# A new issue order for sketched attention with a gated MLP: S2 on the sync queue, copies of S behind the second turn of keys

## The chip, the cores and the metric

The kernel runs on one core of a Trainium2 chip. The metric is the time of one execution on the device in microseconds; lower is better. The engines are named as in the profile: PE is TensorE (matmuls), PEld its weight loads, DVE is VectorE, ACT is ScalarE, POOL is GpSimd, and SP is SyncE, which issues nearly all DMAs. A "q" behind a name is the engine's sequencer.

## The reference

Sixteen pairs of batch and head (4 by 4), 1088 positions, head size 32, all float32. Each row of q and k is sketched by two 8x32 matrices, and the attention is linear in the 64 products:

```python
a = einsum('rd,bhsd->bhsr', S1, x)
b = einsum('rd,bhsd->bhsr', S2, x)
phi(x) = einsum('bhsi,bhsj->bhsij', a, b).reshape(..., 64)
kv  = einsum('bhsf,bhsd->bhfd', phi(k), v)
z   = sum(phi(k), axis=2)
out = einsum('bhsf,bhfd->bhsd', phi(q), kv) / (einsum('bhsf,bhf->bhs', phi(q), z)[..., None] + 1e-06)
```

The result, reordered to 4352 tokens of 128 features, goes through a gated MLP with 2048 hidden units:

```python
h = x @ w_in
g = h * (1.0 / (1.0 + exp(-beta * h)))
result = g @ w_out
```

## The kernel before

Every step of the work is a small function under a short name, put into a table by a decorator: `@op("l2")` or an entry `DO["tk1"]`. A string, SEQ, lists all names in the order in which the instructions are issued, and the last two lines run through it: `for s_ in SEQ.split(): DO[s_]()`. There is no scheduler behind it. Each engine executes its own instructions in just this order and waits at each for its operands and for the buffer that it writes; engines run ahead of one another as far as that allows. So SEQ sets both the queue of each engine and, by the case of a letter, often the engine itself: the same step exists in a form for VectorE (capital) and one for GpSimd or ScalarE (small letter).

The names, with their lines in the profile (a digit 0 to 3 behind a name is the batch b; a second digit a part of it):

- Loads, on SP unless said otherwise: l1 and l2 (S1 and S2, lines 216 and 220, on ACT's queue), lka and lkb (the two halves of the keys of b=0) and lk1 to lk3 (line 148), lq0 to lq3 (queries, 148), lv0 to lv3 (values, 163), lb0 and lb1 (beta, spread over the partitions, 184), li0 and li1 (w_in, 178), lo0 and lo1 (w_out, 192), lp (beta, one column per hidden unit, 224), vz (a memset of a value tile on GpSimd, 175).
- Start: ci and c0 (constants), c1 (head sums of the identity, DVE, 259), h0 and h (one filler matmul on constant data, 128x384, line 267, whose result nobody reads), sm (spread_s: S1 and S2 over the partitions by matmuls, 287 and 294, into one PSUM tile `sps`), sk (masked copies of it, ACT, 305), SW0/SW1 or sw0/sw1 (plain copies of it, DVE or ACT, 317), BS or bs (blocks of S2, DVE or ACT; bs is line 328).
- Keys and queries per batch: tka, tkb, tk1.. and tq0.. (32x32 turns on DVE, 494), kpa, kpb, kp1.. (the projections of the keys, 513), ka (turn of them into `kab`, DVE, 571), o/O (outer products of the keys, `kp`, in five parts, GpSimd or DVE, 536), gr (gram, 586), gc/GC (its copy, ACT or DVE, 597), wp (wprime, 606), wm0, wc/WC (copies of it, 618 and 694), qp and qc0 (projections of the queries, 513, 630 and 703), qa and qd0 (turns into `qab` and `qcc`, DVE, 641, 717 and 648).
- Denominator: DM/dm (product, DVE or GpSimd, 656 and 723), DR (sum, 670 and 732), DI (reciprocal, 674 and 737), DS/ds (scaling of `qab`, 678 and 741). For b=0 a and b are the first two and the other seven of nine groups of columns.
- p/P (outer products of the queries, `qo`, GpSimd or DVE, 536), in parts like o/O. For b=0 they are turned on PE (f0 to f4, line 864) and copied (m/M, ACT or DVE, 878); for the others they are turned on DVE (t, four parts per batch, 757).
- v (sums over the keys, PE, 838 for b=0 and 809), kc and kt (copy or turn of the result, 850 and 821), nd (six small DMAs that deal it out, SP, 507), n0x and n1 to n3 (the numerators, PE, 892 and 772), x/X (their copies to the tokens `xT`, ACT or DVE, 904, 783 and 790).
- MLP weights: u/U (w_in times beta, GpSimd or DVE, 339, four blocks of 512 columns, `winp`), rb (1/beta, DVE, 362), a/g/e (w_out times 1/beta, sixteen blocks, ACT, GpSimd or DVE, 345 and 353, `woutp`).
- MLP: W (1024 columns of h for a chunk of tokens, two or four matmuls, line 400, into one of two PSUM buffers `wave`), S (silu of one W on ACT, 417, into one of 24 tiles g), V (the second product for one W, 447; 435 for the last chunk), y (result out of PSUM, DVE, 470 and 467), z (stores, SP, 376 and 481). There are 68 each of W, S and V; W, S and V take the chunks in order (256, 512, 256, six of 512, 256 tokens), so that the first sixteen W need tokens of b=0 alone.

PSUM is cut into named buffers: two `wave` (two banks each), one `two` (two banks), one `one`, and one accumulator. sps, gram, wprime, kvs and n02 share `one`; kps, the first tile of qps, f1 to f4 and the first tile of n1 to n3 share `two`; the second tiles of qps and n1 to n3, and f0 with n00, take a `wave`. GpSimd can't reach PSUM here: all its steps are products of two SBUF tiles.

Of the kernel before, what the change touches and what calls it, by code (L numbers as in the profile page):

```python
# [19 lines left out]
def kernel(  # L20
# [14 lines left out]
    B, H, S, D = q.shape  # L35
# [50 lines left out]
    def sb(shape, dtype, name):  # L86
        return const.tile(shape, dtype, tag=name, name=name)
# [16 lines left out]
    PE, DVE, ACT, POOL, SP = nc.tensor, nc.vector, nc.scalar, nc.gpsimd, nc.sync  # L104
    DO = {}

    def op(name):
        def put(fn):
            assert name not in DO, name
            DO[name] = fn  # L110
            return fn

        return put
# [11 lines left out]
    sr = sb([R, 2, D], F32, "sr")  # L125
# [12 lines left out]
    sk = sb([P, 2, 2, R], F32, "sk")  # L138
# [78 lines left out]

    @op("l2")
    def load_s2():
        ACT.dma_start(out=sr[:, 1], in_=S2)  # L220

    @op("lp")
    def load_beta_pu():
# [659 lines left out]
    for n, (j0, j1) in enumerate(JRP):  # L883
# [20 lines left out]
                eng(out=xT[:, P * j0 : P * j0 + w], in_=b0["n", n][:, :w])  # L904

    SEQ = """
        ci l2 l1 h0 h h lka c0 tka h lkb h h h h sm h sk h SW0 tkb h kpa c1 h lq0 kpb lk1 lv0 lq1 bs ka0
        SW1 o00 tq0 h h h h gr0 h gc0 h wp0 wm0 o04 qp0 o01 lb0 o03 li0 qc0 tk1 qa0 qd0 DMa h DRa DMb
        o02 DIa DRb kp1 h v00 ka1 dsa v01 p00 h li1 DIb tq1 DSb gr1 gc1 v02 h lb1 h h wp1 f0 P04 P03 wc1
        qp1 P01 M0 v03 qa10 lv1 U0 v04 kc qa11 O10 p02 h u1 lp U3 h n00 f1 x00 f2 W h DM1 W lk2 h m1 m2  # L910
        lo0 n01 U2 S O11 S O14 f3 lo1 W O13 x01 DR1 DI1 rb W o12 v10 S f4 M3 S W v11 tk2 S v12 lk3 v13
        vz m4 v14 lq2 e7 h g0 DS1 W kt1 a1 nd1 g3 W kp2 S n02 g5 e13 g11 W e9 g4 g8 e2 a10 S ka2 V g14
        P10 W x02 e15 gr2 t10 S W S g6 V gc2 W S wp2 V e12 p11 tq2 WC2 t11 S V W qp2 y V qa20 lq3 lv2
        qa21 S p13 o20 W p12 V dm2 t13 V S t12 W W tk3 V V o21 S o22 n1 O24 V S W DR2 X10 o23 v20 v21
        v22 v23 DI2 x11 v24 ds2 S W V S W P20 lv3 kp3 S kt2 nd2 t20 W S V P22 ka3 W gr3 W S y S t22 P21
        V p23 GC3 z W t23 S z V W V t21 V S o30 W O33 S tq3 wp3 y WC3 n2 W S X20 o32 X21 v30 V V W S qp3
        qa30 V qa31 o31 W V V z S W S W S V V DM3 W DR3 V W v31 S v32 W y O34 DI3 S DS3 V W V S S W z
        p30 V W S V S W V W S p32 V W S V W p33 V S t30 y W v33 v34 S W S V W V S p31 S W V t32 t31 W S
        V S W V S kt3 W V W S V t33 V S nd3 y W n3 V X30 S V z V W V V S X31 W W V S V W V z S y W S S V
        W V S W V S W V W V V S W S W V V S S W S V W V S W S V W V W S V S W V y W S V S W S V W V S V  # L920
        V z y V z y z z
    """
    for s_ in SEQ.split():
        DO[s_]()
# [29 lines left out]
```

## Time and profile before

| | us |
|---|---|
| median of 3 runs | 110.5 (110.27 to 114.07) |
| the profiled execution | 110.41 |
| its span, first to last instruction | 108.6 |
| PE busy, share of the span | 97.3 (90%) |
| DVE busy | 64.0 (59%) |
| ACT busy | 71.7 (66%) |
| POOL busy | 35.4 (33%) |

All times in the rows are microseconds from the start of the span. A row of a timeline gives start, length, engine, line, operation, output and inputs, shapes and a count; where several like instructions follow one another they are one row, and its length runs from the first start to the last end. In brackets stands the idle time of the engine before it and what ended it. A row of the chain that ended last gives start, length and what the end of the program hung on at that time. A row of the table by windows gives the window, its length, then the busy time and the number of instructions of PE, PEld, DVE, ACT and POOL, then the granted TensorE clock, the share of the DMA engines and GB/s.

### The profile page before, as it was taken

What the parts mean: (1) busy time and instruction counts of PE and PEld (TensorE: products, weight loads), DVE (VectorE), ACT (ScalarE), POOL (GpSimd) and SP (SyncE); (2) the same over time, 40 slices, a digit from 0 to 9 for tenths busy, and PEclk for the clock granted to TensorE, in tenths of its full rate; (3) what the DMA queues carried; (4) which work ended last, traced back from release to release, by engine and by line L of the source; (5) the groups of instructions that cost most, each with busy time, mean ns of one, the idle gap of its engine ahead of it and who ended that gap; (6) DMA issues with size and microseconds to landing.
All of it is one profiled execution on the core that took longest, in us unless ns stands there. A gap on an engine that the chain in (4) does not pass through costs nothing.

```text
span 108.6 us, 2920 instructions
## 1 busy us (share of the span) xinstructions
PE 97.3 (90%) x1193; PEld 54.8 (50%) x1193; DVE 64.0 (59%) x120; ACT 71.7 (66%) x90; POOL 35.4 (33%) x50
## 2 busy tenths in 40 slices
PE   6798769599996989999999999999999999999930
PEld 3323446185743645655744555555554554556820
DVE  3269999999599999979984844037026220100210
ACT  3230001149897938389946699999991899999900
POOL 5009758800866707794900007900000000000000
PEclk9999999958999999999999999999999999999996
DMA  3999999999201698001354001400025405023061
GB/s 74 351 247 230 368 410 259 240 388 398 88 0 27 187 273 179 4 6 26 61 82 73 0 3 30 66 0 15 15 48 83 79 13 89 0 34 63 0 97 48
DMA packets 23660, 12.64 MB, mean 116 GB/s; under 512 B 19424, under 2 KB 21728, under 8 KB 23648
## 3 DMA queue, kind: packets, MB, share of 16 engines
q1 hardware_dynamic: 23616, 12.47, 44.4%
q8 instruction: 9, 0.15, 0.6%
q14 instruction: 3, 0.02, 0.1%
q10 hardware_dynamic: 32, 0.00, 0.0%
HBM read 9.94 MB, written 2.23 MB: 112 GB/s over the span
## 4 chain that ended last, share of the span: by engine, by line
PE 68%; DVE 21%; issue 3%; DMA 3%; ACTq 1%; DVEq 0%
PE wave L400 27%; PE moeout L447 24%; PE nps L772 4%; DVE woutp L353 4%; DVE qT L494 3%; PE kvs L809 3%; DMA sr<-in_S_dram 3%; PE qfps L864 3%; DVE qo L536 3%; DVE kT L494 2%; DVE kab L571 2%; PE kps L513 2%; PE moeout L435 2%; DVE qm L656 1%; PE kvz L267 1%
## 5 line engine op out<-in xcount | busy, mean ns | idle before, releaser
L417 ACT ACTIVATE g<-wave 128x1024 f16<-128x1024 f32 x68 | 64.9, 1039 | 10.3 <-PE wave L400 10.3
L400 PE MATMUL wave<-xT,winp 128*128 128x512 f16 (+1 forms) x160 | 40.9, 355 | 0.0
L447 PE MATMUL moeout<-g,woutp 128*128 128x512 f16 (+1 forms) x144 | 36.2, 356 | 1.2 <-DVE woutp L353 0.9
L400 PEld LDWEIGHTS <-winp 128*128 128x128 f16 x160 | 21.5, 146 | 12.8 <-issue 1.9
L470 DVE STREAM_TRANSPOSE o_sb<-moeout 128x512 f32<-128x512 f32 (+1 forms) x9 | 5.9, 653 | 27.6 <-PE moeout L447 27.2
L447 PEld LDWEIGHTS <-woutp 128*128 128x128 f16 x144 | 13.4, 97 | 14.2 <-issue 1.9
L536 POOL TENSOR_TENSOR kp<-kab 128x512 f32<-128x512 f32 (+1 forms) x13 | 14.6, 1156 | 8.6 <-DVE qw L317 6.1
L536 POOL TENSOR_TENSOR qo<-qab 128x512 f32<-128x512 f32 (+1 forms) x10 | 12.7, 1291 | 14.3 <-DVE qab L741 11.9
L267 PE MATMUL kvz<-idle 128*128 128x384 f16 x29 | 8.4, 391 | 1.4 <-DVE hm L238 1.1
L757 DVE STREAM_TRANSPOSE qt<-qo 128x512 f32<-128x512 f32 (+1 forms) x12 | 8.7, 745 | 1.2 <-POOL qo L536 1.2
L536 DVE TENSOR_TENSOR qo<-qab 128x512 f32<-128x512 f32 (+1 forms) x7 | 6.8, 996 | 0.9 <-POOL qab L741 0.9
L494 DVE STREAM_TRANSPOSE kT<-k 128x1088 f32<-128x1088 f32 (+2 forms) x5 | 5.4, 1070 | 1.3 <-DMA k<-in_k_dram 1.3
L597 ACT COPY gt<-gram 128x32 f32<-128x32 f32 x3 | 0.6, 184 | 7.8 <-PE gram L586 7.8
L267 PEld LDWEIGHTS <-idle 128*128 128x128 f16 x29 | 2.8, 111 | 4.9 <-issue 3.2
L717 DVE STREAM_TRANSPOSE qab<-qps 128x576 f32<-128x576 f32 x6 | 4.4, 764 | 1.3 <-PE qps L703 1.3
L494 DVE STREAM_TRANSPOSE qT<-q 128x1088 f32<-128x1088 f32 x4 | 5.1, 1285 | 0.0
L772 PE MATMUL nps<-qt,nd 32*32 32x288 f32 x192 | 5.0, 412 | 0.0
L353 POOL TENSOR_TENSOR woutp<-w_out_sb,rbeta 128x128 f16<-128x128 f32 x8 | 2.9, 402 | 6.0 <-DVE rbeta L362 6.0
L353 DVE TENSOR_TENSOR woutp<-w_out_sb,rbeta 128x128 f16<-128x128 f32 x6 | 4.8, 820 | 0.0
L783 DVE CAST xT<-nps 128x576 f16<-128x576 f32 x5 | 3.8, 755 | 1.7 <-PE nps L772 1.4
L536 DVE TENSOR_TENSOR kp<-kab 128x512 f32<-128x512 f32 (+1 forms) x7 | 4.3, 638 | 0.0
L809 PE MATMUL kvs<-kp,v 128*32 128x64 f32 x216 | 4.3, 222 | 0.0
(83 smaller groups left out, 71.5 us busy)
## 6 DMA issues: line engine op xcount, KB each, us to landing
q<-in_q_dram SPq DMA_DIRECT2D x4, 544.0 KB, 4.7
v<-in_v_dram SPq DMA_DIRECT2D x15, 144.0 KB, 6.6
k<-in_k_dram SPq DMA_DIRECT2D x3, 544.0 KB, 7.3
out_dram<-o_sb SPq DMA_DIRECT2D x18, 64.0 KB, 2.0
beta_bc<-in_moe_beta_dram SPq DMA_DIRECT2D x2, 512.0 KB, 9.8
w_in_sb<-in_moe_w_in_dram SPq DMA_DIRECT2D x2, 512.0 KB, 9.0
w_out_sb<-in_moe_w_out_dram SPq DMA_DIRECT2D x2, 512.0 KB, 7.1
k<-in_k_dram SPq DMA_DIRECT2D x1, 288.0 KB, 2.8
```

Of the source, the lines that this page charges most:

```text
L267: PE.matmul(out=kvz[:, P:], lhsT=idle, rhs=cut(idle, [[0, 3], [1, P]]), start=fresh, stop=True, skip_group_check=True,)
L353: eng.tensor_tensor(out=woutp[:, j, :], in0=w_out_sb[:, j, :], in1=cut(rbeta, [[0, P]], j), op=MUL,)
L400: PE.matmul(out=wv[:, jj // per, o : o + tw], lhsT=unit(j0 + jj), rhs=xT[:, t0 : t0 + tw], start=True, stop=True,)
L417: ACT.activation(out=g, in_=wv, func=ACTF.Silu)
L447: PE.matmul(out=moe["acc"][:, :tw], lhsT=woutp[:, j, :], rhs=g[jj], start=(j == 0), stop=(j == NJ - 1),)
L470: DVE.transpose(out=o_sb[:, :nt, :].rearrange("p t d -> p (t d)"), in_=t[:, :tw])
L494: DVE.transpose(out=dst[:, t0:t1].rearrange("p t s -> p (t s)"), in_=src[:, t0:t1].rearrange("p t d -> p (t d)"),)
L536: eng.tensor_tensor(out=cut(dst[b][:, j0:j1], [[F, n], [R, R], [1, R]]), in0=cut(t, [[step, n], [1, R], [0, R]], j0 * H * step), in1=cut(t ...
L717: DVE.transpose(out=cut(QAB[b], [[4 * R, 2], [4 * R * H, NJK], [1, 4 * R]], 2 * 4 * R * n), in_=PS["qps", b][n][:, :, :JW],)
L757: DVE.transpose(out=QT[b][:, j0:j1].rearrange("p j h c s -> p (j h c s)"), in_=QO[b][:, j0:j1].rearrange("p j h f -> p (j h f)"),)
L772: PE.matmul(out=tiles[g // 2][32 * h : 32 * h + 32, g % 2, : 32 * nj], lhsT=nd_of(b, h, fc, g), rhs=QT[b][rows, :nj, h, fc, :], start=(fc ...
L809: PE.matmul(out=KVZ[b][32 * h : 32 * h + 32, :F], lhsT=v_t[b][:, h, j, :], rhs=KP[b][:, j, h, :], start=(j == 0), stop=(j == NJK - 1), ski ...
```

## The change

l2 moves from ACT's DMA queue to SP's, and in SEQ behind lka. The copy SW0 gives way to sw0 on ACT, and SW1 moves behind tkb; BS takes the place of bs. Of 29 fillers h and h0, five stay. All other steps stand in another order, and some change their engine by their letter: on DVE there are now P00, P02, DSa, P12, O22, O24 (earlier), O30, O31, X01, X02, M4, GC2, DS2, e5, e6, e8, e10, e13, e14 and e12; on GpSimd dmb, dsb, p01, o10, o13, o14, o21, o23, o33, o34, p20 to p23, ds3 and g0, g2, g3, g7, g9, g11; on ACT m0, m3, a1, a4, a15, gc3, x10, x11, x20, x21, x30 and x31. No step changes what it computes.

```diff
--- before.py
+++ after.py
@@ -217,7 +217,7 @@
 
     @op("l2")
     def load_s2():
-        ACT.dma_start(out=sr[:, 1], in_=S2)
+        SP.dma_start(out=sr[:, 1], in_=S2)
 
     @op("lp")
     def load_beta_pu():
@@ -904,21 +904,20 @@
                 eng(out=xT[:, P * j0 : P * j0 + w], in_=b0["n", n][:, :w])
 
     SEQ = """
-        ci l2 l1 h0 h h lka c0 tka h lkb h h h h sm h sk h SW0 tkb h kpa c1 h lq0 kpb lk1 lv0 lq1 bs ka0
-        SW1 o00 tq0 h h h h gr0 h gc0 h wp0 wm0 o04 qp0 o01 lb0 o03 li0 qc0 tk1 qa0 qd0 DMa h DRa DMb
-        o02 DIa DRb kp1 h v00 ka1 dsa v01 p00 h li1 DIb tq1 DSb gr1 gc1 v02 h lb1 h h wp1 f0 P04 P03 wc1
-        qp1 P01 M0 v03 qa10 lv1 U0 v04 kc qa11 O10 p02 h u1 lp U3 h n00 f1 x00 f2 W h DM1 W lk2 h m1 m2
-        lo0 n01 U2 S O11 S O14 f3 lo1 W O13 x01 DR1 DI1 rb W o12 v10 S f4 M3 S W v11 tk2 S v12 lk3 v13
-        vz m4 v14 lq2 e7 h g0 DS1 W kt1 a1 nd1 g3 W kp2 S n02 g5 e13 g11 W e9 g4 g8 e2 a10 S ka2 V g14
-        P10 W x02 e15 gr2 t10 S W S g6 V gc2 W S wp2 V e12 p11 tq2 WC2 t11 S V W qp2 y V qa20 lq3 lv2
-        qa21 S p13 o20 W p12 V dm2 t13 V S t12 W W tk3 V V o21 S o22 n1 O24 V S W DR2 X10 o23 v20 v21
-        v22 v23 DI2 x11 v24 ds2 S W V S W P20 lv3 kp3 S kt2 nd2 t20 W S V P22 ka3 W gr3 W S y S t22 P21
-        V p23 GC3 z W t23 S z V W V t21 V S o30 W O33 S tq3 wp3 y WC3 n2 W S X20 o32 X21 v30 V V W S qp3
-        qa30 V qa31 o31 W V V z S W S W S V V DM3 W DR3 V W v31 S v32 W y O34 DI3 S DS3 V W V S S W z
-        p30 V W S V S W V W S p32 V W S V W p33 V S t30 y W v33 v34 S W S V W V S p31 S W V t32 t31 W S
-        V S W V S kt3 W V W S V t33 V S nd3 y W n3 V X30 S V z V W V V S X31 W W V S V W V z S y W S S V
-        W V S W V S W V W V V S W S W V V S S W S V W V S W S V W V W S V S W V y W S V S W S V W V S V
-        V z y V z y z z
+        l1 lka ci l2 h0 c0 sm tka lkb sk h h tkb kpa c1 SW1 kpb BS ka0 lq0 sw0 gr0 gc0 tq0 o00 wp0 lk1
+        wm0 tk1 lv0 qp0 qc0 lq1 h qa0 qd0 DMa DRa h DIa DSa o01 lb0 P00 o04 dmb kp1 ka1 v00 f0 li0 o03
+        o02 gr1 gc1 v01 DRb v02 DIb dsb wp1 tq1 li1 lb1 v03 P02 m0 v04 P03 lk2 P04 wc1 p01 lv1 u1 qp1
+        qa10 kc U0 qa11 n00 f1 o10 x00 lo1 DM1 U2 m1 U3 W S f2 W DR1 m2 DI1 S vz W n01 S o13 W f3 O11 lp
+        o12 X01 DS1 f4 S W m3 tk2 W v10 P10 v11 rb o14 M4 v12 e14 lo0 v13 g11 e13 v14 g9 lq2 e8 lv2 g2
+        g0 S kt1 W e6 e5 a15 kp2 S S a1 g3 ka2 n02 W X02 W t10 V gr2 P12 a4 e10 lk3 g7 S o20 O24 S GC2 W
+        o21 V t12 W V wp2 S e12 tq2 S WC2 W V p13 W nd1 v20 O22 o23 v21 S qp2 v22 t13 y qa20 S v23 p11
+        qa21 v24 W S V V lq3 dm2 t11 W DR2 n1 tq3 S W tk3 kt2 x10 x11 V V V S W V S W kp3 W DI2 S DS2 V
+        z W S V ka3 W S O30 S gr3 O31 y W V nd2 W p20 t20 S V gc3 W o33 V p22 S o32 V z W p21 S o34 wp3
+        W p23 y V V S WC3 W V t23 S S W S t22 lv3 V W V t21 qp3 qa30 S W S qa31 V DM3 V V W n2 S y x20 V
+        x21 DR3 W DI3 V V W V S W S S V ds3 W V p30 W v30 z p33 v31 S S W S V W V W v32 S v33 p32 y v34
+        t30 S z t33 W V W V t32 p31 S W S V t31 z S V W V S W V kt3 W V nd3 S V W S S y W V V W S V n3 S
+        x30 V x31 V W V V S W S V y W S V W V W S V W V S W S V W V S z S W V W S V S W V y W S V W V S
+        W S V S W V S z W V S W V W S V z y W V S S W V V S V y z z
     """
     for s_ in SEQ.split():
         DO[s_]()
```

## The prediction

> **What bounds the kernel now.** I read the page first, then the chain that ended last in order of time, then the timelines of VectorE, GpSimd, ScalarE and TensorE.
>
> ```profile
> PE 68%; DVE 21%; issue 3%; DMA 3%; ACTq 1%; DVEq 0%
> ```
> ```profile
> 5.69 0.62 PE kps L513 x8
> ...
> 7.27 0.22 DVE kab L571
> ...
> 21.48 1.91 PE qfps L864 x8
> ...
> 39.76 0.04 issue
> 39.80 0.59 PE moeout L447 x2
> ...
> 43.43 1.53 PE nps L772 x63
> ...
> 45.93 1.14 PE kvs L809 x72
> ...
> 48.52 0.65 PE kps L513 x16
> ...
> 58.74 0.70 PE qps L703 x32
> ...
> 68.33 0.43 PE moeout L447 x2
> 68.76 0.48 PE wave L400 x2
> ...
> 80.69 1.69 PE nps L772 x53
> ...
> 102.25 1.65 PE moeout L435 x28
> ```
>
> The second column is the length of a piece. Up to 39.76 us most pieces are VectorE's, with a stretch of TensorE's that begins at 21.48; from 39.80 the chain stays on TensorE to 103.90, where only the last copy and store are left. So VectorE sets when TensorE gets full work, and n1 (the numerators of b=1, at 43.43) is the landmark: it needs all of VectorE's turns t10 to t13, and every W from the 17th on needs it.
>
> VectorE's stretch is not all work. These are single instructions of VectorE, then GpSimd's beside them:
>
> ```profile
> 11.88 1.15 DVE L656 TENSOR_TENSOR qm<-qab,qcc 128x64 f32<-128x64 f32 x1
> ...
> 16.89 1.57 DVE L536 TENSOR_TENSOR qo<-qab 128x512 f32<-128x512 f32 x1
> 18.38 1.75 DVE L536 TENSOR_TENSOR qo<-qab 128x512 f32<-128x512 f32 x1
> ...
> 22.62 0.64 DVE L536 TENSOR_TENSOR kp<-kab 128x512 f32<-128x512 f32 x1
> ...
> 24.16 0.68 DVE L339 TENSOR_TENSOR winp<-w_in_sb,beta_bc 128x512 f16<-128x512 f32 x1
> ...
> 28.66 0.69 DVE L878 COPY qf<-qfps 128x512 f32<-128x512 f32 x1 [1.35 <-PE qfps L864]
> ...
> 30.50 0.25 DVE L353 TENSOR_TENSOR woutp<-w_out_sb,rbeta 128x128 f16<-128x128 f32 x1
> 31.37 1.16 DVE L353 TENSOR_TENSOR woutp<-w_out_sb,rbeta 128x128 f16<-128x128 f32 x1
> 32.45 1.59 DVE L353 TENSOR_TENSOR woutp<-w_out_sb,rbeta 128x128 f16<-128x128 f32 x1
> 35.30 1.15 DVE L353 TENSOR_TENSOR woutp<-w_out_sb,rbeta 128x128 f16<-128x128 f32 x1
> ...
> 41.15 1.53 DVE L757 STREAM_TRANSPOSE qt<-qo 128x768 f32<-128x768 f32 x2
> ```
> ```profile
> 11.87 1.08 POOL L536 TENSOR_TENSOR kp<-kab 128x512 f32<-128x512 f32 x1
> ...
> 16.59 1.31 POOL L536 TENSOR_TENSOR qo<-qab 128x512 f32<-128x512 f32 x1 [1.30 <-DVE qab L678]
> 17.88 1.71 POOL L339 TENSOR_TENSOR winp<-w_in_sb,beta_bc 128x512 f16<-128x512 f32 x1
> 19.55 1.52 POOL L536 TENSOR_TENSOR kp<-kab 128x512 f32<-128x512 f32 x1
> ...
> 27.44 2.92 POOL L353 TENSOR_TENSOR woutp<-w_out_sb,rbeta 128x128 f16<-128x128 f32 x8 [6.01 <-DVE rbeta L362]
> ```
>
> A product of 128x512 takes VectorE 0.64 us when GpSimd is idle (22.62) and 1.57 or 1.75 when GpSimd runs one too. The ends tell how: GpSimd's product ends at 17.90 and VectorE's, begun at 16.89, at 18.46, one product's work later; GpSimd's next ends at 19.59 and VectorE's next at 20.13. DMa, 64 elements, began at 11.88 and ended at 13.03, just after GpSimd's at 12.95. So two products of two SBUF operands never overlap, and the engines take turns. Waits of VectorE for that: 0.9 (DMa), 0.9 (P03), 1.1 (P01), 0.9, 1.35 and 0.9 (three scalings e): **6.05 us**. Another 1.35 goes to M3's wait for TensorE. VectorE's turns are done at 41.15+1.53 = 42.68, 0.75 before n1.
>
> **The change, step by step.** I follow VectorE to the turn that releases n1 (now t12, then t11), and then TensorE to the end.
>
> Step 1, the start. Now the first matmul of spread_s waits for S1, whose DMA is issued second.
>
> ```profile
> 1.37 2.93 DMA sr<-in_S_dram
> ```
> ```profile
> 3.53 0.78 DVE L494 STREAM_TRANSPOSE kT<-k 128x576 f32<-128x576 f32 x1 [1.31 <-DMA k<-in_k_dram]
> ```
> ```profile
> 1.06 2.74 PE L267 MATMUL kvz<-idle 128*128 128x384 f16 x8 [1.06 <-DVE hm L238]
> 4.43 0.33 PE L287 MATMUL sps<-ident,sr 8*32 8x8 f32 x16 [0.63 <-DMA sr<-in_S_dram]
> 7.13 0.82 PE L267 MATMUL kvz<-idle 128*128 128x384 f16 x4
> ```
> ```profile
> 1.10:4.50 3.40, 2.77 (x13) 1.09 (x17) 1.48 (x11) 1.49 (x2) 0.91 (x7) 1.00 0.80 260
> ...
> 18.20:21.60 3.40, 1.86 (x33) 0.97 (x30) 3.40 (x5) 0.32 (x2) 3.18 (x3) 1.00 1.08 227
> 21.60:25.00 3.40, 3.40 (x17) 2.86 (x17) 3.40 (x7) 1.84 (x4) 0.00 (x0) 0.50 1.03 394
> ```
>
> S2 goes behind the first half of the keys on SP, which lands at 3.53; S2 can't land before that and, by the 2.93 us of S1's transfer, hardly after 4.3. I take 3.9: 0.5 sooner. SP's later loads each go out one issue later, which no step here waits for; ACT's queue loses the 0.60 us issue. The filler h between the two halves of kps goes: 0.3 more. Against it stands the clock. The eight first fillers take 0.34 us apiece and the four at 7.13 about 0.2, though the clock column (third from the end of the windows) says 1.00 for both: that column knows nothing before its first entry, and TensorE begins at about half pace. The changed order keeps 5 of 29 fillers and one of the first eight, so both halves of kps, 0.62 us each, stream at half pace and take up to 1.1 us more. Sum 7.27-0.5-0.3+1.05: kab starts at **7.5, +0.25** (6.5 at full pace, 8.0 with a late S2). SW0 is gone from in front of the second turn of keys; it sat in VectorE's wait for kps, so nothing comes of it alone. BS takes bs's place on VectorE, between 0.25 and 0.64 us by the products above, in the same wait; I take 0.3, and nothing on the path. sw0 lies in ScalarE's idle time.
>
> Step 2, VectorE's own work up to the turn. It gains P00, P02, P12, O22 (0.64 each), DSa (64 elements, under the 0.25 of 128: 0.2), X01, X02, M4 (0.69 for a full copy; 1.6 together), five other e's (0.25 each), O24 and GC2 (0.5): 6.1. It loses DMb, DSb (224 elements each, 0.7 together), P01, O10, O13 (0.64 each), O14 (0.35), M0, M3 (0.69 each) and four e's (1.0): 5.4. **+0.7.**
>
> Step 3, the turns with GpSimd, which gains dmb, dsb, o10, o13, o14, o21, o23 and loses dsa, p12, two scalings and one product of QO. I walk both queues at 0.6 us for a product on VectorE and 1.0 on GpSimd (1.1 for u1, 1.4 for p13), in turns: DSa waits 0.15 for dmb; P00 1.0 for o03; P02 0.45 for p01; P03 1.1 for u1; P04 0.95 for o10; U0 0.2 for o13; DM1 0.25 for o12; U2 0.6 for o14: 4.7. That puts U3 at 25.9, where the last of winp comes at 24.84 now (24.16+0.68; GpSimd rests for 6.01 us ahead of 27.44 now, so that U0, U2 and U3 run undisturbed). Then five e's among six g's (0.3 each), P12 behind o21 (0 or 0.85, I take 0.4), e10 behind p13 (1.35), O24 behind o23 (0.95): 4.05. Together **8.75 against 6.05, +2.7**; if the meetings miss each other, -1.5; if every one meets a full product, +4.
>
> Step 4, other waits. M3's 1.35 is gone (m3 is ScalarE's). X01 waits for n01, which stands behind W 3, which needs U3: 0 to 1.1 us, I take 0.5. **-0.85.** rb comes at about 31.5 instead of just before 27.44, since tk2 and P10 go first. The first V, which waits for the scalings behind rb, stays near 34 (now the last of these ends at 32.45+1.59), but the fourth waits for e12 at about 41 and TensorE idles some 3 us before that. On SP, nd1 now stands behind lv2 and lk3, and lv2 waits for v14, near 33; its six small DMAs still land well ahead of 45.
>
> So t11 ends at 42.68+0.25+0.7+2.7-0.85 = **45.5**. t11 now stands behind qa20 and qa21 in the order, so n1 follows at once, 2.1 us later than 43.43. TensorE has then done 15 W, 6 V and all of v2; now it is 15 W, 9 V and no v2: 3x0.43 against 1.14, the same amount of work.
>
> Step 5, from n1 to the end; now 103.90-43.43 = 60.5.
>
> ```profile
> 45.81 0.64 ACT L783 CAST xT<-nps 128x576 f16<-128x576 f32 x1 [1.71 <-DVE xT L783]
> ...
> 85.61 7.44 ACT L417 ACTIVATE g<-wave 128x1024 f16<-128x1024 f32 x8 [0.27 <-PE wave L400]
> ```
>
> One S takes 0.93, a W with a V 0.86: where nothing else runs, ScalarE paces, and a W is drawn out from 0.43 to 0.48. The order puts n2 after 31 W and 24 V (now 24 and 16), n3 after 48 and 43 (now 48 and 40). TensorE's sums: n1 to n2 1.53+34x0.43+0.65+0.70 = 17.5; to n3 1.53+36x0.43+1.14 = 18.2; to the end 1.69+45x0.43 = 21.0. ScalarE's, with the five x it newly takes at 0.64 (x11 it has already) and the tail piece of x31, for which I take 0.7: 16.2, 17.1, 21.5. The greater of each and 0.45 for the last V: 57.7. Now TensorE's sum is about 57 against 60.5, 3.5 of friction. With the x copies off VectorE and 8 more V ahead of n2, TensorE paces longer: I take 2, so **59.65, -0.85** (0 to -2). Moving x30 and x31 to ScalarE costs no more there: it idles behind n3 anyway until the copies are done.
>
> Sum: +2.1-0.85 = +1.25 on the profiled execution's 110.41 (span 108.6 and 1.8 around it, 0.1 under the median): **111.6 us**. Its own range, from the bounds of steps 1, 3 and 5, is 110.4 to 113.2.
>
> **Rivals.**
>
> (a) The turns cost no more than now. VectorE's list is full of transposes, under which GpSimd's products are free; that speaks for it. Against: P02 to U3 are six products in a row with little between. Then t11 ends at 42.8, n1 stays at 43.4, step 5 remains: **109.6**.
>
> (b) Faster: the new order feeds TensorE earlier. If GpSimd gets through p01, u1, o10, o13, o12 and o14 under tq1, qa10 and qa11, the 4.7 us shrink to 0.5, X01 waits for nothing and kab starts at 6.75: t11 ends at 42.68-0.5+0.7-1.85-1.35 = 39.7, and n1 follows TensorE's own order, some 1.9 before 43.43. **107.7.** It decides from about four of the eight meetings missed.
>
> (c) Slower still: the clock. With few fillers TensorE idles before f1 (f1 needs qa10) and before V 3 and V 4; 1.86 busy us in the window up to 21.6 were too few to keep the clock, and it was 0.50 for the next 3.4. If it halves again near 42, n1 takes 1.5 more; with kab at 8.0 and X01's full 1.1 that makes +3.7, **114.1**. The Trainium skill's page "TensorE: Matmul & The Clock Gate", Part 1, has the half rate as the state at rest, lifted by one busy window of some 3.4 us and back after an idle one; by it the changed order would start at half rate and fall back wherever V waits. The trace agrees for the 3.4 us at 0.50; how busy is busy enough no row here settles.
>
> **How the numbers follow.** Forecast 0.44, (a) 0.24, (b) 0.16, (c) 0.16. The range 107.9 to 114.2 leaves out most of (b)'s lower half and (c)'s upper half, some 2 in 10. A change under 2% (108.3 to 112.7) is about what a measurement of this kernel can't tell from none. Faster than that: (b) and the low edge of (a), 0.18. Slower: (c) and a third of the forecast, 0.30. Within: 0.52.
>
> **What would show it.** In the changed profile: spread_s near 3.9 and kab near 7.5 (step 1); P00, P03 and P04 drawn out to 1.5 us and ending just after a GpSimd product (step 3); U3 near 26, rb near 31 (step 4); n1 near 45.5 with TensorE idle before the fourth V; ScalarE full from then on (step 5). I am wrong if P02 to U3 take 0.6 us each, or if TensorE is at full pace at 5 us.

## The result and the profile after

The changed kernel is slower. Its median is 115.53 us (114.9 to 118.45, 4 runs) where the kernel before, run beside it, has 110.48 (110.27 to 114.07); the ratio is 1.043, 95% interval 1.037 to 1.049. Run again beside the kernel before it gave 1.026 (1.013 to 1.040) and 1.030 (1.025 to 1.035). So it costs 3 to 4%, where 111.6 us and "within 2%" were forecast. The medians are over all executions of a kernel and the ratios over the fast ones alone, so a ratio is not the quotient of two medians.

The execution that was profiled first took 118.45 us, 2.9 above its median. The chain that ended last and TensorE's timeline of the changed kernel show where it stood still:

```profile
PE 61%; DVE 17%; DMA 9%; issue 5%; ACT 2%; SPq 2%; DVEq 0%
```
```profile
2.49 8.92 DMA k<-in_k_dram
11.41 0.02 issue
11.43 1.31 DVE kT L494
```
```profile
22.28 1.20 PE L703 MATMUL qps<-qT,qw 32*32 32x288 f32 x12
26.07 1.23 PE L703 MATMUL qps<-qT,qw 32*32 32x288 f32 x20 [2.59 <-issue]
```

TensorE stands still for 2.59 us within one group of 32 matmuls; neither of the two other profiles of this kernel has that stop. What all three share are two waits of VectorE for loads at the start, for the queries of b=0 and for the second batch of keys (those of b=1): 1.37 and 1.17 us here, 0.68 and 0.86 in e1, 1.91 and 0.55 in e15. In the chain above the second keys are in transit until 11.41, and 9% of the span now hangs on DMAs, 3% before.

I therefore read the change from another execution of the same kernel, 114.16 us (run e15 below). First VectorE in the kernel before, then the chain of e15, its VectorE and its TensorE:

```profile
7.27 0.85 DVE L571 STREAM_TRANSPOSE kab<-kps 128x288 f32<-128x288 f32 x2 [0.71 <-PE kps L513]
...
8.10 1.29 DVE L494 STREAM_TRANSPOSE qT<-q 128x1088 f32<-128x1088 f32 x1
...
9.45 1.30 DVE L494 STREAM_TRANSPOSE kT<-k 128x1088 f32<-128x1088 f32 x1
```

```profile
PE 52%; DVE 27%; DMA 10%; issue 3%; ACT 3%; SPq 2%; DVEq 0%
...
47.45 1.53 PE nps L772 x63
...
67.17 1.53 PE nps L772 x63
...
86.07 1.53 PE nps L772 x63
...
106.49 1.95 DMA out_dram<-o_sb
108.45 0.49 DVE o_sb L467 x2
```
```profile
6.86 0.85 DVE L571 STREAM_TRANSPOSE kab<-kps 128x288 f32<-128x288 f32 x2 [0.81 <-PE kps L513]
9.62 1.31 DVE L494 STREAM_TRANSPOSE qT<-q 128x1088 f32<-128x1088 f32 x1 [1.91 <-DMA q<-in_q_dram]
...
11.56 1.31 DVE L494 STREAM_TRANSPOSE kT<-k 128x1088 f32<-128x1088 f32 x1 [0.55 <-DMA k<-in_k_dram]
...
14.83 1.03 DVE L678 TENSOR_TENSOR qab<-qab,rc 128x64 f32<-128x64 f32 x1
15.89 1.46 DVE L536 TENSOR_TENSOR qo<-qab 128x512 f32<-128x512 f32 x1
...
19.86 4.21 DVE L536 TENSOR_TENSOR qo<-qab 128x512 f32<-128x512 f32 x3
...
27.02 1.72 DVE L339 TENSOR_TENSOR winp<-w_in_sb,beta_bc 128x512 f16<-128x512 f32 x2
...
33.28 0.24 DVE L362 RECIPROCAL rbeta<-beta_pu 128x16 f32<-128x16 f32 x1
...
38.24 1.15 DVE L353 TENSOR_TENSOR woutp<-w_out_sb,rbeta 128x128 f16<-128x128 f32 x1
```
```profile
3.78 0.29 PE L287 MATMUL sps<-ident,sr 8*32 8x8 f32 x8 [1.27 <-DMA sr<-in_S_dram]
...
5.32 1.48 PE L513 MATMUL kps<-kT,sk 64*32 64x288 f32 x16
...
56.65 0.60 PE L447 MATMUL moeout<-g,woutp 128*128 128x256 f16 x4 [0.63 <-DVE o_sb L470]
```

The reader should see that the start up to `kab` is quicker than before (6.86 against 7.27), that VectorE then waits 1.91 and 0.55 us for the loads of q and k, for which it did not wait before, and that everything behind comes as much later: n1 at 47.45 instead of 43.43. From n1 to the last copy it is 61.0 us, 60.5 before.

### The profile page after: what moved, and what is told of

Its sections match the earlier page's. It is cut to its first block, busy times and chain, and to the rows that moved or that the text cites. A ratio compares the mean times of both kernels' runs of the same rounds, so it can differ in the third digit from the quotient of the medians.

```text
span 116.7 us, 2827 instructions
## 1 busy us (share of the span) xinstructions
PE 100.2 (86%) x1169; PEld 56.2 (48%) x1169; DVE 60.0 (51%) x112; ACT 75.3 (65%) x93; POOL 37.4 (32%) x52
## 4 chain that ended last, share of the span: by engine, by line
PE 61%; DVE 17%; DMA 9%; issue 5%; ACT 2%; SPq 2%; DVEq 0%
PE wave L400 22%; PE moeout L447 21%; DMA k<-in_k_dram 8%; PE nps L772 4%; PE qps L703 3%; PE kvz L838 3%; DVE woutp L353 3%; PE qfps L864 3%; PE kvs L809 3%; DVE qo L536 3%; ACT g L417 2%; DVE kp L536 2%; DMA out_dram<-o_sb 2%; DVE kab L571 1%; DVE kT L494 1%
## 5 line engine op out<-in xcount | busy, mean ns | idle before, releaser
L400 PE MATMUL wave<-xT,winp 128*128 128x512 f16 (+1 forms) x160 | 42.1, 363 | 0.1
L536 POOL TENSOR_TENSOR kp<-kab 128x512 f32<-128x512 f32 (+1 forms) x15 | 15.7, 1061 | 8.1 <-DVE kab L571 7.8
L536 POOL TENSOR_TENSOR qo<-qab 128x512 f32<-128x512 f32 (+1 forms) x11 | 13.5, 1235 | 4.1 <-DVE qab L741 4.0
L703 PE MATMUL qps<-qT,qw 32*32 32x288 f32 x96 | 4.5, 593 | 2.6 <-issue 2.6
L353 POOL TENSOR_TENSOR woutp<-w_out_sb,rbeta 128x128 f16<-128x128 f32 x6 | 2.4, 437 | 10.0 <-DVE rbeta L362 10.0
L864 PE MATMUL qfps<-ident,qo 128*128 128x128 f32 x18 | 4.1, 378 | 1.3 <-DVE qo L536 1.3
L536 DVE TENSOR_TENSOR kp<-kab 128x512 f32<-128x512 f32 (+1 forms) x5 | 5.2, 1053 | 0.0
L783 ACT CAST xT<-nps 128x576 f16<-128x576 f32 x6 | 3.8, 638 | 2.0 <-PE nps L772 1.9
L809 PEld LDWEIGHTS kvs<-kp,v 128*32 128x32 f32 x216 | 3.7, 122 | 2.4 <-issue 1.5
L571 DVE STREAM_TRANSPOSE kab<-kps 128x288 f32<-128x288 f32 x8 | 3.4, 456 | 2.7 <-PE kps L513 2.7
```

The lines of the kernel that those rows point to most:

```text
L353: eng.tensor_tensor(out=woutp[:, j, :], in0=w_out_sb[:, j, :], in1=cut(rbeta, [[0, P]], j), op=MUL,)
L400: PE.matmul(out=wv[:, jj // per, o : o + tw], lhsT=unit(j0 + jj), rhs=xT[:, t0 : t0 + tw], start=True, stop=True,)
L536: eng.tensor_tensor(out=cut(dst[b][:, j0:j1], [[F, n], [R, R], [1, R]]), in0=cut(t, [[step, n], [1, R], [0, R]], j0 * H * step), in1=cut(t ...
L703: PE.matmul(out=tiles[h // 2][32 * g : 32 * g + 32, h % 2, :JW], lhsT=qw[b % 2][rows].rearrange("p n r -> p (n r)"), rhs=q_of(b, rows, g), ...
L809: PE.matmul(out=KVZ[b][32 * h : 32 * h + 32, :F], lhsT=v_t[b][:, h, j, :], rhs=KP[b][:, j, h, :], start=(j == 0), stop=(j == NJK - 1), ski ...
L864: PE.matmul(out=t[:, o : o + P], lhsT=QO[0][:, j, 2 * m : 2 * m + 2, :].rearrange("p h f -> p (h f)"), rhs=ident, is_transpose=True, start ...
```

## The experiments

### The clock and the fillers

e1 is the changed kernel unaltered. e2 puts the 24 dropped fillers back into it, e3 takes them out of the kernel before:

```diff
# e2, SEQ of the changed kernel: h back at the 24 places of before
-        l1 lka ci l2 h0 c0 sm tka lkb sk h h tkb kpa c1 SW1 kpb BS ...
+        l1 lka ci l2 h0 h h c0 h h h h h sm tka lkb sk h h tkb kpa h c1 SW1 kpb h h h h BS ...
# e3, SEQ of before: five h left, as in the changed kernel
-        ci l2 l1 h0 h h lka c0 tka h lkb h h h h sm h sk h SW0 tkb h kpa ...
+        ci l2 l1 h0 lka c0 tka lkb sm h sk h SW0 tkb kpa ...
```

> The changed kernel once more, for a second profile. If its waits for the queries and for the keys of b=1 (1.37 and 1.17 us of VectorE) and the 2.6 us in which TensorE stops in the middle of the projection of the queries of b=1 belong to the order, they are here again; if they belong to the one execution profiled, they are gone and the time is near 115.4.

> The changed order with the 24 fillers put back where they stood. Clock theory (TensorE at half pace until 32 us is most of the loss): the clock is full from about 5 us, the first W comes some 3 us sooner, 111 to 112.5. Turn theory (products of VectorE and GpSimd that take turns, and the late scalings, are most of it): 114.5 to 116, since VectorE sets the pace.

> The order of before, with the same 24 fillers taken out and nothing else. Clock theory: TensorE stays at half pace through the first 20 to 30 us, 113 to 115. Turn theory: VectorE sets the pace all the same, 110.5 to 111.5.

e1 gave 114.77 (113.77 to 118.2), e2 115.95 (ratio to before 1.042, 1.029 to 1.055; e1's is 1.026, 1.013 to 1.040), e3 110.15 (0.989, 0.975 to 1.002). Fillers gain nothing in the new order and taking them out costs nothing that can be told in the old. So the part of rival (c) that rests on the fillers falls. What a full clock at the start would give, e2 does not show: its granted clock is 0.50 from 18.10 to 24.90 all the same, and there five fillers take 1.96 us while VectorE waits 2.48 for the matmuls behind them. That the time hangs little on the half rate at the start is read from e15: between the turn of the second keys and n1 the profile lists a single wait of VectorE, 0.42 for TensorE (X01).

### The loads at the start

e4 makes only the first half of the change in the old order: S2 on the sync queue behind lka, the copies of S behind tkb. e5, and again e16 beside e15 (the changed kernel once more), undoes it in the new order:

```diff
# e5, e16: the changed kernel
-        SP.dma_start(out=sr[:, 1], in_=S2)
+        ACT.dma_start(out=sr[:, 1], in_=S2)
-        l1 lka ci l2 h0 c0 sm
+        l2 l1 lka ci h0 c0 sm
```

> The order of before with the named parts of the change alone: S2 on the sync queue behind the first half of the keys, the copies of S behind the second turn of keys. If the start gains what I forecast (S2 half a microsecond sooner): kab at about 6.7 and 109.7 to 110.5. If S2 in the sync queue holds up the queries and the keys of b=1: 110.8 to 112.

> The changed kernel with S2 back on ScalarE's queue, in front of S1; all else as changed. Theory L (S2 ahead of the other loads in the sync queue makes them late, and the new order has no slack for it): q's and k's second turns wait for no DMA, w_in's issue is back at about 7.0 us instead of 8.9, qd0 ends near 12 instead of 13.6, n1 begins near 45.4 instead of 47.0, the time falls by 1.5 against the changed kernel (to about 113.3 where that is 114.8). Rival O (only the order of the steps counts; the same edit in the old order moved nothing): the early waits go, but the turns with GpSimd and TensorE's waits take the gain back, n1 stays within 0.4 of 47.0, and the time within 0.4 of the changed kernel's.

> The changed kernel once more, beside the next one. Theory Q (S2 in the sync queue makes the loads behind it late): w_in's issue near 8.9 and the second keys turned at 11 or later, here and not in the next run. Rival H (the loads are late in some executions with S2 in either queue): both spread over the same 9.7 to 11.8, and the medians of the two differ by 0.5 at most.

> The changed kernel with S2 back on ScalarE's queue, once more. Theory Q: w_in's issue near 7.7, the second keys turned near 9.8 without a wait, time 1 below the changed kernel's. Rival H: keys between 9.7 and 11.8 as chance has it, time within 0.5 of the changed kernel's.

e4: 111.33 (110.06 to 114.87, 10 runs) beside 111.37 of the kernel before, no difference that can be told. e5: 113.69, ratio 1.032 (1.027 to 1.036). e15 and e16 on one chip: 113.94 and 113.55, ratios 1.030 (1.025 to 1.035) and 1.020 (1.013 to 1.027). VectorE and the chain in e5, then in e16:

```profile
9.75 1.31 DVE L494 STREAM_TRANSPOSE kT<-k 128x1088 f32<-128x1088 f32 x1 [0.27 <-DMA k<-in_k_dram]
```
```profile
45.98 1.53 PE nps L772 x63
```
```profile
10.49 1.31 DVE L494 STREAM_TRANSPOSE kT<-k 128x1088 f32<-128x1088 f32 x1 [1.03 <-DMA k<-in_k_dram]
```
```profile
46.38 1.53 PE nps L772 x63
```

With S2 back on ScalarE's queue the second keys are turned at 9.75 and 10.49 and the profiled executions take 112.72 and 113.12, against 113.77 and 114.16 of e1 and e15: 1.05 less both times. That is the size that theory Q named, but it rests on single executions, and e1 and e5 ran on different chips. In the medians S2 on ScalarE's queue is worth less: 0.4 (e16 beside e15), within rival H's 0.5, and 0.6 (e5 beside e7 of the same rounds, a version of the changed kernel that is no quicker than it). Where the turn of the second keys began right at the end of a wait for their load, it did so at 9.75 to 11.82 in six profiles with S2 on ScalarE's queue (e5, e12, e16, e18, e11, e9; 10.78 on average) and at 10.39 to 11.56 in seven with S2 on SP's (e10, e7, e1, e6, e17, the first profile, e15; 11.13 on average). So the landing wanders by 2 us from execution to execution, as rival H had it, and what S2 in front adds, anything up to about 1 us, can't be told from that here. The issue alone is 0.35: the first load of v goes out at 2.97 instead of 2.62 in SP's queue. The Trainium skill's page "DMA: Bandwidth & Descriptors", section "Queues, rings and completion order", says that each of the two queues has a ring of its own on the same 16 DMA engines and that an engine takes a ring's descriptors in order. By that, S2 on the sync queue stands behind the first keys and ahead of the other large loads, and on ScalarE's beside them; no run here shows the rings themselves.

e13 and e14 make the loads late on purpose, in the new and the old order:

```diff
+    @op("ld")
+    def load_dose():
+        SP.dma_start(out=w_out_sb[:, :4, :], in_=...)   # 256 KB, loaded again by lo0
# SEQ
-        lq0
+        ld lq0
```

> The changed kernel with one more load of 256 KB on the sync queue in front of lq0 (the first quarter of w_out, loaded again later): it makes q, the second keys and all behind them later, and computes nothing. Theory D (the new order passes a late load on to the end): the second keys are turned about 1 us later than in the changed kernel (near 12), n1 comes 35.9 after that turn begins, and the time grows by as much as the keys are late, about 1. Rival S (the order has slack behind the loads; the loss is elsewhere): the keys are late, n1 and the time grow by 0.3 at most.

> The kernel before with the same extra load in front of lq0. Theory D (the old order holds n1 by TensorE's list and hides up to 2 us of lateness): the second keys are turned at 10.5 to 12, n1 stays at 43.0 to 43.8 and the time within 0.4 of the kernel before. Rival S (both orders pay alike; the earlier spread was chance): n1 and the time grow by as much as the keys are late, about 1.

e13: 115.12, ratio 1.040 (1.034 to 1.047), 1.2 above e15's median on the same chip. e14: 111.67, 0.8 above the median of the kernel before in the same rounds (110.83) and inside its spread, with no ratio; its profiled execution took 110.72. So that the old order hides the extra load is seen in that one execution and not shown by the times. VectorE and the chain of e13 (the lines are 7 higher than elsewhere), then of e14:

```profile
12.13 1.31 DVE L501 STREAM_TRANSPOSE kT<-k 128x1088 f32<-128x1088 f32 x1 [1.08 <-DMA k<-in_k_dram]
...
46.50 1.45 DVE L724 STREAM_TRANSPOSE qab<-qps 128x576 f32<-128x576 f32 x2 [0.71 <-PE qps L710]
```
```profile
49.17 1.53 PE nps L779 x63
```
```profile
11.02 1.31 DVE L501 STREAM_TRANSPOSE kT<-k 128x1088 f32<-128x1088 f32 x1
```
```profile
43.22 1.53 PE nps L779 x63
```

In the new order the keys come 0.57 later than in e15 and n1 1.72. The rest, 1.15, falls where TensorE is at half rate, as the windows of e13 and then of e15 show in the third column from the end:

```profile
43.40:46.80 3.40, 3.40 (x88) 1.88 (x90) 2.69 (x6) 1.29 (x2) 0.23 (x1) 0.50 0.45 157
```
```profile
43.40:46.80 3.40, 3.31 (x112) 2.30 (x113) 3.40 (x6) 1.50 (x2) 0.18 (x1) 1.00 0.31 103
```

The 32 matmuls of qps b=1 take 1.27 at half rate and 0.77 in e15, and VectorE waits 0.71 for them. What rival (c) put "near 42" is met in three of the twelve profiles of the new order, e10 left out (the first one at 45.8 to 49.2, e2 at 42.5 to 45.9, e13 at 43.4 to 46.8), each time behind an idle time of 1.35 of TensorE, which waits for GC2's copy of gram ahead of wps. That idle time is there in six more, e1 and e15 among them, without the half rate. In the old order the dose is not seen as a wait, since `kab` came late anyway; the keys are turned 1.57 later than in the first profile of before, and n1 begins 0.21 earlier.

The start of the second keys' turn and that of n1, for the old order in all profiles and for the new one in those with VectorE's list as changed and full clock from 29 us on:

| order | turn of keys → n1 (difference) |
|---|---|
| old | before 9.45 → 43.43 (33.98); e3 10.02 → 43.61; e12 10.20 → 43.34; e18 10.71 → 43.00; e8 10.99 → 43.58; e14 11.02 → 43.22; e4 11.33 → 43.06 (31.73) |
| new | e5 9.75 → 45.98 (36.23); e16 10.49 → 46.38 (35.89); e7 10.97 → 46.85 (35.88); e1 11.17 → 47.05 (35.88); e17 11.22 → 47.09 (35.87); e15 11.56 → 47.45 (35.89) |

The old order begins n1 between 43.0 and 43.6 whenever the second keys are turned, over 1.9 us of lateness, whether the keys landed late (e12, e18) or `kab` came late (e4, e8, e14). The new one begins it 35.9 after them, to 0.02 us from 10.5 on; in e5, with the earliest turn, X01 waits 0.78 for TensorE instead of 0.42, which is the 0.34 more. Left out are the first profile (40.27, with the stop of 2.59), e2 (10.30 → 48.86, 38.56, with the wait of 2.48 behind fillers) and e13 (37.04), all three with half rate near 42, e10, and e6, e9 and e11, where VectorE's list is shorter (below). e4's VectorE shows what gives way in the old order:

```profile
13.77 0.47 DVE L656 TENSOR_TENSOR qm<-qab,qcc 128x64 f32<-128x64 f32 x1
...
28.43 0.63 DVE L878 COPY qf<-qfps 128x512 f32<-128x512 f32 x1
...
31.30 1.79 DVE L353 TENSOR_TENSOR woutp<-w_out_sb,rbeta 128x128 f16<-128x128 f32 x3
...
40.78 1.53 DVE L757 STREAM_TRANSPOSE qt<-qo 128x768 f32<-128x768 f32 x2
```

DMa (13.77) takes 0.47 instead of 1.15, and M3 (28.43) waits for TensorE no longer, where it waited 1.35 before: 2.0 us given back for 1.9 lost. Behind it three scalings that took 2.84 take 1.79, and other products that meet GpSimd's take 1.0 more.

### The turns with GpSimd

e6 gives e10 and e12 to ScalarE in the new order; e8 moves five scalings ahead of GpSimd's long products in the old:

```diff
# e6, SEQ of the changed kernel
-        a4 e10 lk3 g7 S o20 ... wp2 S e12 tq2
+        a4 a10 lk3 g7 S a12 o20 ... wp2 S tq2
# e8, SEQ of before: e13 e9 e2 e15 e12 leave their places
-        lq2 e7 h g0
+        lq2 e7 e13 e9 e2 e15 e12 h g0
```

> The changed kernel with the scalings e10 and e12 of w_out done by ScalarE (behind a4 and behind the next S), no longer by VectorE. Theory T (VectorE's list up to t11 sets n1, the waits in turn with GpSimd included): VectorE loses 1.15 and 0.42 of work and wait, GC2 comes 1.1 sooner, n1 1.0 to 1.5 sooner (45.5 to 46.0), the time falls by about 1.0 (113.8 where the changed kernel is 114.8). Rival P (TensorE's and ScalarE's list sets n1, or the wait moves on to another product): n1 moves by 0.3 at most, the time by 0.3 at most.

> The kernel before with VectorE's five scalings e13, e9, e2, e15, e12 directly behind e7, where GpSimd runs short scalings, instead of among GpSimd's long products. Theory T (turns with GpSimd lengthen VectorE's list, and that list sets n1): VectorE saves about 3 us of its waits of 0.9 to 1.35, n1 comes 1 to 2 sooner (41.5 to 42.5 instead of 43.4), the time falls by 1 to 1.5 (about 109.3 where the kernel before is 110.5). Rival P (TensorE's own order sets n1 once the scalings are done): n1 moves by less than 0.5 and the time by less than 0.5.

e6: 112.23 (111.96 to 112.48), ratio 1.018 (1.014 to 1.021), 2.1 below e7 of the same rounds, a version of the changed kernel that is no quicker than it (below). Its profiled execution is 1.54 below e1's. VectorE and TensorE of e6, then VectorE of e8:

```profile
11.18 1.31 DVE L494 STREAM_TRANSPOSE kT<-k 128x1088 f32<-128x1088 f32 x1 [1.15 <-DMA k<-in_k_dram]
```
```profile
45.30 1.72 PE L772 MATMUL nps<-qt,nd 32*32 32x288 f32 x64
```
```profile
31.89 1.26 DVE L353 TENSOR_TENSOR woutp<-w_out_sb,rbeta 128x128 f16<-128x128 f32 x6
...
37.92 0.17 DVE L694 COPY qw<-wps 128x8 f32<-128x8 f32 x1 [0.71 <-PE wps L606]
...
40.12 1.45 DVE L717 STREAM_TRANSPOSE qab<-qps 128x576 f32<-128x576 f32 x2 [0.80 <-PE qps L703]
```

n1 comes 1.5 to 1.7 sooner in e6 than in e7 and e1 (45.30 by the timeline against 46.78 and 46.98): theory T holds in the new order. The loads have no part in it: the second keys are turned at 11.18 in e6 and at 11.17 in e1, and from there to e10 VectorE's instructions start within 0.05 us of each other in the two. TensorE's idle time ahead of wps is gone with it, and the six runs of e6 lie within 0.5 of each other, where e7's reach from 113.97 to 117.72; that the half rate makes this difference is likely from the windows above, and not shown. In the old it fails: e8 does six scalings in 1.26 us, but VectorE then waits 0.71 and 0.80 for TensorE, n1 begins at 43.58 and the time is 110.22, ratio 0.998 (0.995 to 1.001). In that execution `kab` came 1.4 late (8.68), so it is the ratio of twelve executions, more than the profile, which says that the scalings weren't what the time hung on there; rival P holds.

### Behind n1

e7 moves the second chunk's y ahead of ka3; e10, and e17 again, give the copies x10, x20, x21, x30 and x31 back to VectorE:

```diff
# e7
-        z W S V ka3 W S O30 S gr3 O31 y W V nd2
+        z W S V y ka3 W S O30 S gr3 O31 W V nd2
# e10, e17
-        kt2 x10 x11 V ... S y x20 V x21 DR3 ... n3 S x30 V x31 V
+        kt2 X10 x11 V ... S y X20 V X21 DR3 ... n3 S X30 V X31 V
```

> The changed kernel with the turn y of the second chunk ahead of ka3 and O31 instead of behind them. Theory Y (the changed order puts y behind the turn of keys and a product on VectorE, and V 13 waits for the bank that y frees; that is a part of the gain that step 5 of the prediction lacks): TensorE's idle 0.64 ahead of V 13 (at 56.25) goes, n1 to the last copy takes 60.4 instead of 61.0, the time falls by 0.5. Rival P (ScalarE paces from there on and takes the lead back): the wait goes, n1 to the last copy stays at 61.0, the time within 0.2.

> The changed kernel with the copies x10, x20, x21, x30, x31 done by VectorE again, as before the change. Theory F (behind n1 the lost time is V 13's wait for y, the change-overs of TensorE and ScalarE's pace, which the x copies don't set): n1 to the last copy stays at 61.0 within 0.3, the time within 0.3. Rival A (five more copies of 0.64 keep ScalarE from its S and TensorE from its W and V): n1 to the last copy falls by 1 or more, to 60.0 at most, the time by 1.

> The changed kernel with x10, x20, x21, x30 and x31 on VectorE again, as before the change. Theory F (the friction behind n1 is V 13's wait for y and the change-overs, not the x copies): n1 to the last copy 61.0 within 0.3, time within 0.4 of the changed kernel's. Rival A (the copies keep ScalarE from its S): n1 to the last copy 60.0 at most, time 1 lower.

e7: 114.32, ratio 1.035 (1.031 to 1.040). The wait for y goes and a new one comes; TensorE of e7:

```profile
55.62 0.38 PE L586 MATMUL gram<-kab 128*32 128x32 f32 x18 [1.11 <-DVE kab L571]
```

y could not start before 54.12, when TensorE had done V 12, and `kab`, whose matmuls were done at 52.2, now stood behind it. From n1 to the last copy it took 61.4 us, no less than 61.0. So y belongs behind ka3, as in e11 below.

e10: 117.2, ratio 1.047 (1.033 to 1.060); its profiled execution took 224.76 us, with TensorE at about half pace throughout, and tells nothing about the copies. e17: 116.23, ratio 1.054 (1.046 to 1.062). Both theories fail: n1 to the last copy takes 62.9 us (47.09 to 109.99), 1.9 longer than with the copies on ScalarE. The chain in e17 shows how:

```profile
50.13 0.65 DVE xT L783
...
50.87 0.65 ACT xT L783
```

x10 stands on VectorE behind two turns of 1.3 and starts 1.4 after n1 is done, x11 follows on ScalarE, and TensorE's next W waits 1.04 for them. The copies on ScalarE are a gain of the change, about 2 us against the same order without them.

### Together

e9 makes three edits to the changed kernel: S2 on ScalarE's queue, e10 and e12 on ScalarE, rb (with lp) directly behind DI1. e11 adds y between ka3 and O30. e12 and e18 take the kernel before without its 24 fillers and with e8's order.

```diff
# e11
-        z W S V ka3 W S O30 S gr3 O31 y W V nd2
+        z W S V ka3 y W S O30 S gr3 O31 W V nd2
```

> The changed kernel with three edits: S2 on ScalarE's queue again, e10 and e12 done by ScalarE, and rb (with its load lp) in front, right behind DI1. Theory A (start, VectorE's turns and the stretch behind n1 are terms that add): by the two edits apart, -1.05 and -1.55 in their profiled executions, n1 begins near 44.4 and the last copy at 105.4, span 109.4, time near 111.2; rb in front lets V start earlier, which is worth nothing to n1 or up to 0.5. Rival O (the gains overlap: TensorE becomes the bound ahead of n1): n1 stays above 45.0 and the time above 111.8.

> The three edits at once, and y of the second chunk directly behind ka3, ahead of the products O30 and O31. Theory Y (V 13 waits for y behind the two products; put in front of them, y costs the turn of keys nothing, unlike in the run where it stood ahead of ka3): TensorE waits neither for y nor for kab at 53 to 56, n1 to the last copy takes 60.4, the time is 0.5 below that of the three edits alone. Rival P (ScalarE's list behind it takes the lead back): within 0.2 of the three edits alone.

> The kernel before without its 24 dropped fillers and with the five scalings directly behind e7. Rival P to the turns (in the old order TensorE's own list is the bound from 25 us on, so nothing on VectorE's list moves the end): 110.4 within 0.5, as with each edit alone. Theory T: each edit was masked by the other's wait, together they give 1 us (109.4).

> The kernel before without its 24 dropped fillers and with its five scalings directly behind e7, again. If the first five rounds told the truth: 0.989 of the kernel before, 109.2 where that is 110.4, the interval below 1. If they were chance: 1.000 within 0.005, as the two edits apart.

e9: 0.997 of before (0.989 to 1.005); e11: 0.999 (0.993 to 1.006). The whole loss is gone. One of the twelve executions of e9, which left no profile, took 421.98; the others lie between 109.75 and 113.87. VectorE of e9, and the chain of e11 (its n1 is at 45.35):

```profile
11.82 1.31 DVE L494 STREAM_TRANSPOSE kT<-k 128x1088 f32<-128x1088 f32 x1 [1.74 <-DMA k<-in_k_dram]
```
```profile
45.35 1.67 PE nps L772 x62
...
64.51 1.53 PE nps L772 x63
...
102.74 0.73 DVE o_sb L470
...
105.78 0.51 DVE o_sb L467 x2
```

In the executions that were profiled the keys were late again, at 11.82 and 11.70, with S2 on ScalarE's queue, so n1 misses the 44.4 of theory A: it comes at 45.45 and 45.35, 33.6 behind the keys instead of 35.9. In e11 n1 to the last copy takes 60.43, the 60.4 of theory Y, and TensorE waits neither for y nor for `kab`; the time of e11 can't be told from that of e9.

e12: 110.03, 0.989 (0.979 to 0.9996). e18, the same kernel: 110.49, 0.994 (0.988 to 1.0004). The best version here gains about half a per cent on the kernel before, at the edge of what these rounds can tell.

## Why the prediction was wrong

By its own terms, for the execution of 114.16 us (e15):

| term | predicted | measured |
|---|---|---|
| turn of the second keys begins | 9.45 + 0.25 = 9.7 | 11.56 |
| from there to n1 | 45.5 - 9.7 = 35.8 | 35.89 |
| n1 to the last copy | 59.65 | 61.00 |
| last copy to the end of the span | 4.68 | 3.95 |
| around the span | 1.8 | 1.76 |
| sum | 111.6 | 114.16 |

**Step 1 failed**, in the sentence "SP's later loads each go out one issue later, which no step here waits for". Its own edits came as said or better: the second matmul of spread_s at 3.78 (3.9 forecast), `kab` at 6.86 (7.5). The clock was misread there: the 0.62 us of each half of `kps` was taken for full pace and 1.05 more put down, but 16 such matmuls take 0.65 at 48.52 in the kernel before and 0.72 at 34.40 in e15, so those of before ran at about half pace too, and the new 1.48 is 0.24 more. But the turns of q and k behind `kab` wait for their loads, 2.46 us together, and this ate the quick start and 1.86 more, which n1 followed one to one. I had one execution of before, in which the keys happened not to be waited for; that VectorE turned them at 9.45 told that they had landed by then, not with how much to spare. Two things can stand behind the 1.86: S2 in front of the loads, worth anything up to about 1 us (e5, e16), and a landing that varies by 2 us with S2 in either queue; how it divides is not shown. e5, with S2 back on ScalarE's queue, is the execution in which the second keys were turned when the forecast had it, at 9.75: there n1 began at 45.98 (45.5 forecast) and the time was 112.72. Of the 1.1 that it is above 111.6, 0.5 lies ahead of n1 and the rest behind it (step 5 and the end).

**Steps 2 to 4 were right in their sum**, 35.89 against 35.8, and partly by compensation. The turns came near their forecast, some dearer and some cheaper: DSa waited 0.8 instead of 0.15, P00 0.85 instead of 1.0, P02 to P04 took 4.21 where 4.3 was counted, and e10 took 1.15 where 0.25 and a wait of 1.35 were. The end of U3 comes 17.2 behind the keys where 16.2 was forecast (28.74, and 25.9 from 9.7), and the stretch from there to n1 is 0.9 shorter. X01 waited 0.42 (0.5 forecast), rb came 21.7 behind the keys (21.8). Rival (a), that the turns cost no more, and (b), that most meetings are missed, are out; e6 shows that 1.6 us of VectorE's list are 1.6 us of n1.

**The reading of before was half right.** VectorE's list does set n1 in the new order. In the old it doesn't: with the scalings sped up (e8) or the keys 1.9 late (e4) n1 stays at 43.0 to 43.6, because VectorE's list and TensorE's are balanced there, and each has waits that shrink when the other is late (M3's 1.35 in e4; in e8 VectorE's new waits of 0.71 and 0.80). The sum started from an n1 that had 2 us of slack ahead of it and ended on one that has none. Since the sum was made for a single execution, this slack had no term in it.

**Step 5 was mis-sized**: 59.65 forecast, 61.00 measured. The sums of work stand; the friction, "now 3.5", of which I kept 2, is 3.35 (61.00 less 57.65). The gain that I had seen is there (1.9 us for the copies, e17), but the new order gave it back: 0.63 of it where V 13 waits for y behind a turn of keys and two products (56.65), and the rest in places that no run tells apart. The order of e11 takes 60.43. On the other side 0.73 came back at the end, which had no term. Half of it is the issue of the last stores, 0.3 behind the start of the last copies in e15 and 0.67 in the kernel before; the other half lies behind that issue and is not explained:

```profile
108.75 1.32 SPq L481 DMA_DIRECT2D out_dram<-o_sb  x2
```
```profile
104.59 1.33 SPq L481 DMA_DIRECT2D out_dram<-o_sb  x2
```

**Rival (c)** was put at 114.1 and lay nearest. Fillers gain nothing (e2, e3) and VectorE waits only 0.42 for TensorE behind the keys (e15), so the half rate at the start is not what it cost; the late keys are. The half rate "near 42" is there in e2, e13 and the first profile, behind the idle time that (c) named, and costs 1.15 in e13; six others have that idle time and keep the full rate, so that it doesn't fall back wherever V waits. It may explain a part of the distance between the best runs (113.6) and the median of 115.53, which is not shown, as those executions left no profile; it doesn't explain the 3 us of e1 and e15, whose clock is full from 27 on. Two sums of the prediction are off by 0.15 each, which changes nothing: the second part of step 3 adds up to 4.2 and not 4.05, and rival (c) to +3.85 and not +3.7.

## What to carry to other kernels

Before an order is taken over for its sum of work, ask of each load what waits for it and how long it had landed by then: an instruction that waits for nothing in one profile says only that its load was in time once. Two orders with the same work differ in slack: here the one in which two engines' lists are balanced, with waits on both, hid 1.9 us of lateness that the tight list passed on one to one. A tiny load that is moved to the front of a queue puts off the issue of the large ones behind it, here by 0.35 us, so move it only where the loads behind it have room.

## What the hardware showed that I had not expected

- The landing of the same load in the same code varies: the turn of the second keys, held up by the load alone, began at 9.75 and 10.49 in two executions of one kernel (e5, e16), and at 11.82 and 11.70 with the same start in e9 and e11.
- A DMA of 1 KB ahead of the large loads put off their issue by 0.35 us. The end came 1.05 later in two pairs of profiled executions (112.72 and 113.12 against 113.77 and 114.16) and 0.4 and 0.6 later in the medians, which the wandering of the landing leaves undecided.
- TensorE stopped for 2.59 us between two matmuls of one group, with no wait that the profile shows. It is in one profiled execution of the changed kernel and in neither of the other two. An instruction transfer of 0.02 MB ran in the same microsecond, at 23 to 24; one ran in the other two as well, at 25 to 26 in e1 and at 22 to 23 in e15, without a stop. The cause is open.
- In one execution, of 224.76 us (e10), TensorE ran at about half pace from end to end, though the clock column says 1.00: a matmul of W takes 0.73 us on average where e15 has 0.35, and n1's 1.53 is drawn out to 2.97. The other engines kept theirs (an S of ScalarE's 1.02 against 1.05, VectorE's turn of the second keys 1.31 in both). The other executions of this kernel took 115.3 to 119.5.
